# Old-form tiles, tile pairs by seven products, and the denominators of a fused attention and MLP kernel

## The chip, the cores and the metric

The kernel runs on one core of a Trainium2 chip. The metric is the device time of one execution, in microseconds (us). The engines are TensorE (PE in the profile; its weight loads are PEld), VectorE (DVE), ScalarE (ACT), GpSimd (POOL) and SyncE (SP), which here only issues DMAs.

## The reference

A linear attention with positive random features, and on its output an MLP with a gate. q, k and v are 8 x 8 x 576 x 64 (batch, heads, rows, head width), omega is 128 x 64, x has 4608 tokens of 512, the hidden width is 1536.

```python
    def phi(x):
        proj = np.einsum('bhsd,md->bhsm', x, omega)
        sq = np.sum(x * x, axis=-1, keepdims=True) / 2.0
        h = proj - sq
        h = h - np.max(h, axis=-1, keepdims=True)
        return np.exp(h) / np.sqrt(m)
    q_p, k_p = (phi(q_s), phi(k_s))
    kv = np.einsum('bhsm,bhsd->bhmd', k_p, v)
    z = np.sum(k_p, axis=2)
    num = np.einsum('bhsm,bhmd->bhsd', q_p, kv)
    den = np.einsum('bhsm,bhm->bhs', q_p, z)[..., None] + 1e-06
...
    g = x @ w_gate
    silu = g * (1.0 / (1.0 + np.exp(-g)))
    val = x @ w_val
    return (silu * val @ w_out).astype(np.float32)
```

## The kernel before

*Precision.* Each wide matmul of the MLP is three: its two operands are split into a rounded high part and a remainder (hi and lo, both 32 bits wide), and hi by hi, hi by lo and lo by hi are summed in PSUM. A split is a copy to hi on ACT and a subtraction to lo, on POOL for weights and hidden values, on DVE for x.

*Attention.* A group is 256 rows of one pair of heads; a batch has 9, the last of which holds the remaining 64 rows of all four pairs. A step n works on two groups: one of q and one of k, but two of k in the first 6 steps and two of q from step 66 on; there are 72 steps. What a step does, and where:

- `st_transpose`: PE transposes the rows (tile `pt`, L376), ACT copies the result to `x` (L384), POOL squares the rows for their norms (`sq`, L383).
- `st_project`: 16 products with omega (L399) into two PSUM banks, `pp0` and `pp1`.
- `st_max`: DVE sums the squares (L410), takes the maxima of `pp` (L417) and makes the bias `st` (L419, L420).
- `st_exp`: eight exponentials on ACT (L431) read `pp` and `st` and write the features `ph`.
- `k_accumulate`: features of k by v (L534), summed over a batch in `kvacc`. v has a 65th column of ones, so the denominators' vector z comes with it.
- `q_transpose` (`ptq`, L558, copied to `qt` on ACT), `q_mult` and `q_out`: the output of a q group. For batches below `BPOOL` = 4, `q_mult` multiplies `qt` by the 65 columns of kv (`po`, L575); DVE divides by the 65th (`xn`), and `q_out` transposes `xn` back (`xt`, L606). From batch `BPOOL` on, the denominators leave PE: POOL multiplies the features by a broadcast z (`q_den`: `jk`, L490 and L494), DVE sums and inverts, POOL scales the features (`q_norm`, L510) before they are transposed, and `q_out` writes the transposed output at once (`xt`, L613).
- behind either, x of a tile is split from PSUM into `xt[j]` in SBUF (L632 on ACT, L633 on DVE).

*PSUM.* There are eight banks of 128 x 512: four for the MLP (`ps_m`, and `pt` and half of `pp` in the first 25 steps), two in `ps_p` that `pp0`, `pp1`, `pt` and `xt` share in turn from step 25 on, one for `ptq`, `po` and the like, one for `kvacc`. Behind the attention the last four become `ps_w`, for the seven products.

*MLP.* The tokens are 9 tiles of 512, the hidden width 12 blocks of 128. In the **old form** the unit is a visit, one tile by a set of three blocks: 36 matmuls of 128x512 for the gates, 36 for the values (L647) and 36 for the sum into the output (`down`, L656; L680 adds it to `acc` on DVE), 108 in all. A tile takes four visits. `ROUNDS` gives tiles that are worked on together, so that a set of weights, once split, serves two or three tiles: (0, 1, 2), (3, 4), (5, 6), 28 visits. Tiles 7 and 8 go as a **pair** behind them (`last_round`): the pair and two blocks make a 2 x 2 product of blocks, done by seven products (L832) of sums and differences of weights (`load_seven`) and of x (`make_t`) in place of eight. Such a product is six matmuls of 128x512; a pair has six of these longer visits, with 2 x 7 x 6 = 84 of them and 48 of `down`. Their results are joined by L877 and L860 on DVE.

*Order.* All instructions are issued by one Python program, and each engine runs its own in that order. Up to step 25 the parts of a step follow in the order `CLOSE`, then in the order `GROUPED`, which has six slots `SHARE`. In a slot the generator `stream()` is drawn on for MLP work, until what was given has caught up with a curve, `course`. That curve is drawn like a rubber band between `upper` (MLP work whose x is there) and `lower` (work that must be done so that buffers of x, `NXB` pairs of them, come free), and ends `MARGIN` us short of all old-form work that can be had by then. Weights are read, unpacked (POOL, L278), split and stored to DRAM once, in `tick()`s spread over the steps by `marks`, and read from there later (`load_weights`).

The order of a step from the 25th on:

```python
    GROUPED = (
        st_project, q_transpose, lambda n: k_accumulate(n, 0),
        lambda n: k_accumulate(n, 1), st_max, st_exp, q_den,
        SHARE, SHARE, SHARE,
        lambda n: q_norm(n + 1), lambda n: st_transpose(n + 1), q_out, q_mult,
        SHARE, SHARE, SHARE,
    )
```

Of the kernel before, what the change touches and what calls it, by code (L numbers as in the profile page):

```python
# [23 lines left out]
def kernel(  # L24
# [11 lines left out]
    nc = tc.nc  # L36
# [40 lines left out]
    BPOOL = 4  # L77
# [162 lines left out]
    def new_weights(f, i, pool=None):  # L240
        hi, lo = (
            (pool or wpool).tile([P, DM], F32R, name=f"w{e}{f}_{i}", tag=f"w{e}{i}") for e in ("hi", "lo")
        )
        weights[f, i] = hi, lo
# [51 lines left out]
    def load_weights(f, i, pool=None):  # L296
        need(f, i)
        new_weights(f, i, pool)
# [164 lines left out]
    def load_z(n):  # L463

        for _, b, g, gr in slots(n, "q"):
            if g == 0 and b >= BPOOL:
                assert len(converted) == 3 * NF, "the raw weights' buffers are still needed"
                zt = att.tile([P, 2, 4, M], F32, name=f"zt{b}", tag="stw")
# [125 lines left out]

    xt = {}
    cols_done = [0]

    def q_out(n):
        n -= OLAG
        for _, b, g, gr in slots(n, "q"):  # L600
# [24 lines left out]
            for src, pr, j, o, w in parts_:  # L625
                if j not in xt:

                    while j - NXB >= 0 and not finished(j - NXB):
                        assert give(1), "the MLP waits for x, and x for the MLP"
# [28 lines left out]
    at_visit = [0]  # L658

    def finished(j):  # L660

        return at_visit[0] > last_visit[j]

# [5 lines left out]
    def down(j, k_, ht, wts, next_set, tt):  # L669
# [11 lines left out]
        if k_ == (NPF if j >= LASTA else NSET) - 1:  # L681
# [7 lines left out]
    def stream():  # L689

        todo = []
        for vi, (j, s_, k_) in enumerate(visits):
# [26 lines left out]
            if final:  # L719
                load_seven(0, 0)  # L720
# [17 lines left out]
            if final:  # L738
                load_seven(0, 1)
            at_visit[0] = vi + 1  # L740
# [3 lines left out]
        yield from last_round(todo)  # L744
# [10 lines left out]

    late_pools = {}
    sevens = {}
    ts = {}

    def load_seven(pf, i):  # L760

        win = late_pools["win"]
        raws_ = []
        for f in (2 * pf, 2 * pf + 1):
            raw = moe.tile([P, DM], F32, name=f"wraw{f}_{i}s", tag="wraw", bufs=3)
            nc.sync.dma_start(raw, wscr[f, i])
            raws_.append(raw)
        (a11, a12), (a21, a22) = ((r[:, 0:G], r[:, G:DM]) for r in raws_)
        s = win.tile([P, 4, G], F32, name=f"s{pf}_{i}", tag="s")
# [273 lines left out]
```

## Time and profile before

| what | value |
|---|---|
| runs | 1228.45, 1230.39, 1232.96 us; median 1230.39 |
| the profiled execution | 1232.11 us, of which the span, first to last instruction, is 1229.9 |
| granted clock of TensorE | 0.989, mean of the span |
| POOL's low halves of hidden values, L734 | 84 x 1319 ns |
| POOL's squares, L383 | 72 x 1066 ns |
| DVE's maxima, L417 | 144 x 684 ns |
| HBM | 80.02 MB read, 18.89 MB written |

The span in stretches: length, then the busy time of PE, PEld, DVE, ACT and POOL with the number of instructions, the granted clock, the busy share of the 16 DMA engines and GB/s.

```profile
0.00:25.00 25.00, 14.21 (x83) 11.90 (x84) 10.77 (x21) 9.76 (x25) 9.85 (x27) 0.78 0.66 158
25.00:145.00 120.00, 113.35 (x993) 101.56 (x993) 93.79 (x232) 91.77 (x274) 45.77 (x40) 0.95 0.57 143
240.00:1010.00 770.00, 765.27 (x4184) 618.89 (x4183) 324.81 (x627) 374.98 (x789) 346.73 (x289) 1.00 0.25 69
```

The first stretch is the start, before PE has work to do without waiting. The second has the steps in the order `CLOSE`. The third has the attention from some 10 steps behind that, with much MLP work in each step. The old form behind the attention begins near 1010, the pair's stage near 1050.

How to read rows: `L399 PE MATMUL pp<-omT,x ... x16 [2.47 <-ACT ph L431]` is a line, an engine, an operation, the tile written and the tiles read, with how many instructions, and in brackets how long the engine was idle ahead of it and which instruction it waited for. In the order of time, the first two numbers are the start and the length in us.

### The profile page before, as it was taken

The page shows a single profiled execution, that of the slowest core. Times are in us where ns is not written, and L with a number is a line of the kernel's source. Part 1 is how long each engine was busy: PE and PEld are TensorE (multiplying, and loading weights), DVE is VectorE, ACT ScalarE, POOL GpSimd, SP SyncE. Part 2 cuts the span into 40 slices and gives each one's busy share as a digit, 9 for nine tenths or more (in the row PEclk, how much of TensorE's full clock was granted, in tenths as well). Part 3 has the DMA queues.
Part 4 walks back from the last instruction along what each step waited for, and adds up shares of the span by engine and source line. Part 5 has one row for each costly group of instructions (what it writes and reads, how often), then busy time and mean ns, then how long its engine had stood idle before and what let it go on. Part 6 is the DMA issues. An engine that isn't in the chain of part 4 may idle for free. (4 is left out here: it accounts for less than half of the span.)

```text
span 1229.9 us, 18546 instructions
## 1 busy us (share of the span) xinstructions
PE 1193.3 (97%) x6777; PEld 978.9 (80%) x6777; DVE 607.8 (49%) x1192; ACT 624.6 (51%) x1387; POOL 549.3 (45%) x469
## 2 busy tenths in 40 slices
PE   6999999899999999999999999989999999999998
PEld 5888788688888888878888877877777787788886
DVE  4688767436556523433344434432334276545544
ACT  3778766543544425455754556434654423654431
POOL 3424333353444521335544654335556334656541
PEclk7899999999999999999999999999999999999999
DMA  6545644424326312232222221222111113321102
GB/s 148 138 121 141 177 137 142 117 78 142 90 68 181 90 35 73 61 78 61 72 62 61 78 56 44 61 51 60 46 42 43 43 43 77 96 52 52 52 18 69
DMA packets 158986, 100.13 MB, mean 81 GB/s; under 512 B 119824, under 2 KB 132144, under 8 KB 158896
## 3 DMA queue, kind: packets, MB, share of 16 engines
q1 hardware_dynamic: 158896, 98.95, 30.1%
q8 instruction: 54, 0.88, 0.3%
q14 instruction: 36, 0.29, 0.1%
HBM read 80.02 MB, written 18.89 MB: 80 GB/s over the span
## 5 line engine op out<-in xcount | busy, mean ns | idle before, releaser
L431 ACT ACTIVATE ph<-pp,st 128x128 f32<-128x128 f32 x576 | 158.6, 382 | 31.8 <-DVE st L420 30.9
L249 POOL TENSOR_TENSOR wlo<-wraw,whi 128x512 fp32r<-128x512 f32 x93 | 121.8, 1319 | 107.5 <-ACT whi L248 107.1
L383 POOL TENSOR_TENSOR sq<-nat 128x512 f32<-128x512 f32 x72 | 76.7, 1066 | 191.9 <-DMA nat<-in_k_dram 143.2
L680 DVE TENSOR_TENSOR acc<-o,acc 128x512 f32<-128x512 f32 x124 | 84.6, 687 | 116.5 <-PE o L656 116.2
L656 PE MATMUL o<-whi,hh 128*128 128x512 f32 x336 | 135.5, 403 | 3.8 <-ACT hh L733 2.0
L647 PE MATMUL v<-xh,whi 128*128 128x512 f32 x336 | 134.5, 400 | 0.7 <-DVE acc L680 0.7
L647 PE MATMUL g<-xh,whi 128*128 128x512 f32 x336 | 134.6, 401 | 0.0
L656 PE MATMUL o<-whi,hl 128*128 128x512 f32 x336 | 132.3, 394 | 2.3 <-POOL hl L734 2.3
L647 PE MATMUL g<-xl,whi 128*128 128x512 f32 x336 | 131.7, 393 | 0.5 <-DVE xl L633 0.5
L656 PE MATMUL o<-wlo,hh 128*128 128x512 f32 x336 | 131.6, 392 | 0.0
L647 PE MATMUL v<-xh,wlo 128*128 128x512 f32 x336 | 131.4, 391 | 0.0
L647 PE MATMUL g<-xh,wlo 128*128 128x512 f32 x336 | 131.3, 392 | 0.0
L647 PE MATMUL v<-xl,whi 128*128 128x512 f32 x336 | 131.2, 391 | 0.0
L734 POOL TENSOR_TENSOR hl<-sl,hh 128x512 fp32r<-128x512 f32 x84 | 110.5, 1319 | 41.8 <-ACT hh L733 41.3
L417 DVE TENSOR_REDUCE st<-pp 128x4 f32<-128x512 f32 x144 | 93.5, 684 | 54.2 <-PE pp L399 54.2
L733 ACT CAST hh<-sl 128x512 fp32r<-128x512 f32 x84 | 52.1, 626 | 108.7 <-DVE sl L730 108.5
L248 ACT CAST whi<-wraw 128x512 fp32r<-128x512 f32 x93 | 57.4, 625 | 92.2 <-PE v L647 54.1
L410 DVE TENSOR_REDUCE st<-sq 128x8 f32<-128x512 f32 x72 | 49.1, 682 | 105.0 <-POOL sq L383 105.0
L399 PE MATMUL pp<-omT,x 64*128 64x128 f32 x1152 | 98.3, 296 | 2.4 <-ACT x L384 1.2
L399 PEld LDWEIGHTS pp<-omT,x 64*128 64x128 f32 x1152 | 81.2, 196 | 22.8 <-issue 13.9
L730 DVE TENSOR_TENSOR sl<-v,sl 128x512 f32<-128x512 f32 x84 | 57.3, 686 | 72.3 <-PE v L647 70.0
L494 POOL TENSOR_TENSOR jk<-ph,zt 128x512 f32<-128x512 f32 x32 | 41.1, 1290 | 103.6 <-ACT ph L431 86.8
(200 smaller groups left out, 2448.3 us busy)
## 6 DMA issues: line engine op xcount, KB each, us to landing
wraw<-wscr SPq DMA_DIRECT2D x93, 256.0 KB, 2.7
wscr<-wc SPq DMA_DIRECT2D x36, 256.0 KB, 2.2
out_dram<-acc SPq DMA_DIRECT2D x72, 128.0 KB, 2.4
nat<-in_k_dram SPq DMA_DIRECT2D x64, 128.0 KB, 3.3
v<-in_v_dram SPq DMA_DIRECT2D x64, 128.0 KB, 3.4
nat<-in_q_dram SPq DMA_DIRECT2D x64, 128.0 KB, 2.7
st<-in_moe_w_gate_dram SPq DMA_DIRECT2D x12, 512.0 KB, 5.1
st<-in_moe_w_val_dram SPq DMA_DIRECT2D x12, 512.0 KB, 4.4
```

The costliest lines, as they stand in the source:

```text
L248: nc.scalar.copy(hi, raw)
L249: nc.gpsimd.tensor_tensor(lo, raw, hi.bitcast(F32), op=ALU.subtract)
L383: nc.gpsimd.tensor_tensor(sq, nat, nat, op=ALU.mult)
L399: nc.tensor.matmul(pp[hh][:, i, c, :], x[r, i, c * P : (c + 1) * P], omT[r], start=True, stop=True)
L417: nc.vector.tensor_reduce(st[:, 1, :, :, hh], pp[hh], axis=AX.X, op=ALU.max, negate=True)
L431: nc.scalar.activation(ph[:, c, hh * M : (hh + 1) * M], pp[hh][:, i, c, :], AF.Exp, bias=st[:, 3, i, c, hh : hh + 1], scale=1.0,)
L647: nc.tensor.matmul(ps, a_[:, ws], b_[:, c, :], start=n == 0, stop=n == 3 * NC - 1)
L656: nc.tensor.matmul(ps, a_[:, ts_], b_, start=first and n == 0, stop=last and n == 2)
L680: nc.vector.tensor_tensor(a_, po, a_, op=ALU.add)
L730: nc.vector.tensor_tensor(h, pv, h, op=ALU.mult)
L733: nc.scalar.copy(hh, h)
L734: nc.gpsimd.tensor_tensor(hl, h, hh.bitcast(F32), op=ALU.subtract)
```

## The change

1. *Old form and pairs.* `ROUNDS` keeps tiles 0 to 2, 12 visits. Tiles 3 and 4, 5 and 6, 7 and 8 become three pairs by seven products, one behind the other, all behind the attention (`pair_rounds` in place of `last_round`). `MARGIN` goes from 25 to 45 us, and `course` has no lower bound any more.
2. *x of the pairs.* `q_out` copies x of tiles 3 to 8 from PSUM to `xo` (ACT) and stores it to DRAM (`x_dram`), in place of the split into SBUF. The first pair's is read back and split in chunks of 128x512 by `first_x`, in front of the rest of the old-form work behind the attention. A later pair's is read back and added up in the second visit of the pair ahead of it (`next_x`), and split, 128x1024 at a time, in the second half of that pair's last visit (`split_x`), each factor behind the product that reads its predecessor.
3. *Buffers.* The factors' high and low parts have one buffer each. Hidden values, sums and products of the pairs use the buffers of x, of the old form and of `acc`. `NXB` is 3; the broadcast z has a buffer of its own. The products come in the order 1, 5, 6, 3, 7, 2, 4, as before; blocks go forward in the first and third pair and backward in the second, so that a change of pairs needs no new weights.
4. *Denominators.* `BPOOL` goes from 4 to 2: batches 2 and 3 (18 q groups) take the way by POOL too.

```diff
-    ROUNDS = [range(0, 3), range(3, 5), range(5, 7)]
-
-    LASTA, LASTB = 7, 8
+    ROUNDS = [range(0, 3)]
+    PAIRS = [(j, j + 1) for j in range(3, len(TILES), 2)]
     NPF = NF // 2
-    MARGIN = 25.0
-    NXB = 4
+    MARGIN = 45.0
+    NXB = 3
...
-    BPOOL = 4
+    BPOOL = 2
...
         upper[n] = cum[vi] if n > whole[1] else 0.0
-        lower[n] = max([0.0] + [cum[last_visit[j - NXB] + 1] for j in begun if j >= NXB and begun[j] <= n])
-    lower = np.minimum(lower, upper)
...
-                zt = att.tile([P, 2, 4, M], F32, name=f"zt{b}", tag="stw")
+                zt = att.tile([P, 2, 4, M], F32, name=f"zt{b}", tag="zt")
...
+    x_dram = {j: dram.tile([P, NPAIR, T], F32, name=f"xs{j}") for pair in PAIRS for j in pair}
...
+                if j in x_dram:
+                    xo = att.tile(list(src.shape), F32, name=f"xo{b}_{g}_{j}", tag="xo", bufs=3)
+                    nc.scalar.copy(xo, src)
+                    nc.sync.dma_start(x_dram[j][:, pr, o : o + w], xo)
+                    continue
...
+    ORDER = (1, 5, 6, 3, 7, 2, 4)
+    ORDER_B = [PROD[n][1] for n in ORDER]
...
+    def next_x(r):
+
+        for half, names in ((0, ("b11", "t1")), (1, ("b21", "b22"))):
+            for j, name in zip(PAIRS[r], names):
+                nc.sync.dma_start(ahead[name], x_dram[j][:, half * CH : (half + 1) * CH, :])
+        yield
+        for o, a, b in (("t3", "b22", "t1"), ("t1", "t1", "b11"), ("t2", "b22", "t1"), ("t4", "b21", "t2")):
+            for c in range(CH):
+                nc.vector.tensor_tensor(ahead[o][:, c], ahead[a][:, c], ahead[b][:, c], op=ALU.subtract)
+                yield
...
+    def split_x(name):
+        hi, lo = factors[name]
+        nc.scalar.copy(hi, ahead[name])
+        nc.vector.tensor_tensor(lo, ahead[name], hi.bitcast(F32), op=ALU.subtract)
...
+        for vi, (r, k_, pf) in enumerate(pair_visits):
+            then = pair_visits[vi + 1] if vi + 1 < len(pair_visits) else None
+            new_w = then and then[2] != pf
+            new_x = then and then[0] != r
+            if k_ == 1 and r + 1 < len(PAIRS):
+                prep = next_x(r + 1)
...
+                for n in ORDER:
+                    product({5: c, 3: c, 2: d}.get(n, a), n, wts, n in (1, 5, 2))
...
+                    if new_x and i == 1:
+                        split_x(PROD[n][1])
+                    yield US7
+                    if n in (5, 3, 2, 4) and one_down():
+                        yield MM2
...
-    late_pools["mt"] = make_t()
-    for _ in late_pools["mt"]:
-        give(1.0)
+    new_factors()
+    for _ in first_x():
+        give(1.5)
```

What this does to the order of instructions is shown at three places. A line number of the changed kernel can differ from that of before for the same code by 3 to 8 here (L396 and L399 are both the projections).

**First place: PE, step 51, between its projections and the next step's.** `pp` are the projections, `ptq` the transposes of q's features, `kvacc` the k features by v, `pt` the next step's transposes, `xt` an output group; `g`, `v` and `o` are MLP work. Before:

```order
L399 MATMUL pp_51_6225<-omT,x_6165 128x128
L558 MATMUL ptq_7_6234<-ident,ph_49_5950 128x128 x4
L534 MATMUL kvacc_0_6090<-v_95,ph_49_5955 128x65 x4
L647 MATMUL v_6_6269<-xh_2566,whi_1_5971 128x512
L647 MATMUL v_7_6287<-xh_2566,whi_1_5995 128x512
L376 MATMUL pt_6301<-ident,nat_5909 128x128 x4
L613 MATMUL xt_6_6311<-qt_6_6088,kvr_1_4781 64x256 x2
L647 MATMUL v_8_6321<-xh_2566,whi_1_6037 128x512
L647 MATMUL g_6_6339<-xh_4864,whi_0_5878 128x512
L399 MATMUL pp_52_6359<-omT,x_6306 128x128
```

Of each `v` and `g` the first of twelve matmuls is shown. Now:

```order
L396 MATMUL pp_51_4664<-omT,x_4621 128x128
L656 MATMUL o_1_3_4713<-whi_2_3660,hl_5_4387 128x512
L647 MATMUL v_3_4743<-xh_1600,whi_1_3202 128x512
L554 MATMUL ptq_8_4774<-ident,ph_50_4561 128x128 x4
L530 MATMUL kvacc_0_4551<-v_96,ph_50_4566 128x65 x4
L647 MATMUL v_4_4818<-xh_1600,whi_1_3250 128x512
L373 MATMUL pt_4726<-ident,nat_4435 128x128 x4
L611 MATMUL xt_6_4736<-qt_6_4549,kvr_1_3488 64x256 x2
L647 MATMUL v_4_4818<-xh_1600,wlo_1_3251 128x512
L396 MATMUL pp_52_4764<-omT,x_4731 128x128
```

Before, 24 MLP matmuls stood ahead of the transposes `pt` and 24 behind them. Now 13 stand right behind the projections, 2 between `kvacc` and `pt`, and 3 ahead of the next projections.

**Second place: DVE in the half visit at a pair's end.** `c`, `a` and `d` are the products' PSUM banks, `o` that of `down`. Before, in a half visit of the one pair (`sl` are the gates' and hidden values):

```order
L877 TENSOR_TENSOR c_1_10776<-c_1_10736,u_1_10768 128x512
L860 TENSOR_TENSOR sl_1_10617<-c_1_10776,sl_1_10617 128x512
L680 TENSOR_TENSOR acc_1_10526<-o_1_1_10781,acc_1_10526 128x512
L877 TENSOR_TENSOR c_3_10795<-a_1_10735,m_1_10752 128x512
L860 TENSOR_TENSOR sl_3_10619<-c_3_10795,sl_3_10619 128x512
L877 TENSOR_TENSOR c_0_10806<-d_1_10737,m_1_10744 128x512
L860 TENSOR_TENSOR sl_0_10616<-c_0_10806,sl_0_10616 128x512
L680 TENSOR_TENSOR acc_2_10557<-o_1_2_10811,acc_2_10557 128x512
L860 TENSOR_TENSOR sl_2_10618<-a_1_10735,sl_2_10618 128x512
```

Now, where the first pair ends; L923 are the sums, L905 the hidden values, L674 the additions to `acc`, L813 the splits, in which `late` is a full factor:

```order
L813 TENSOR_TENSOR b11lo<-late_7492,b11hi 128x1024
L674 TENSOR_TENSOR acc_0_7901<-o_4_0_8857,acc_0_7901 128x512
L813 TENSOR_TENSOR t1lo<-late_7492,t1hi 128x1024
L923 TENSOR_TENSOR late_7496<-c_1_8837,late_7496 128x512
L813 TENSOR_TENSOR t2lo<-late_7493,t2hi 128x1024
L905 TENSOR_TENSOR sl1k<-late_7496,sl1k 128x512
L813 TENSOR_TENSOR b22lo<-late_7493,b22hi 128x1024
L813 TENSOR_TENSOR t3lo<-late_7494,t3hi 128x1024
L813 TENSOR_TENSOR b21lo<-late_7494,b21hi 128x1024
L905 TENSOR_TENSOR sl2k<-a_1_8836,sl2k 128x512
L813 TENSOR_TENSOR t4lo<-late_7495,t4hi 128x1024
```

Seven splits stand between the evacuations; all but `t4lo` are ahead of the one of bank `a` (`sl2k`).

**Third place: POOL where the third batch's q groups begin.** `sq` are the squares, `wc` an unpacked weight. Before:

```order
L278 TENSOR_TENSOR wc_0_2318<-st_0_2211,wc_0_2318 128x512
L734 TENSOR_TENSOR hl_2_2189<-sl_2_2001,hh_2_2188 128x512
L383 TENSOR_TENSOR sq_2449<-nat_2147 128x512
L278 TENSOR_TENSOR wc_1_2424<-st_1_2316,wc_1_2424 128x512
L383 TENSOR_TENSOR sq_2558<-nat_2256 128x512
```

Now:

```order
L490 TENSOR_TENSOR jk_1_1966<-ph_25_1828,zt_1802 128x512
L506 TENSOR_TENSOR ph_25_1828<-ph_25_1828,dj_1_1968 128x512
L380 TENSOR_TENSOR sq_2243<-nat_1926 128x512
L275 TENSOR_TENSOR wc_0_2102<-st_0_1991,wc_0_2102 128x512
L490 TENSOR_TENSOR jk_2_2094<-ph_26_1956,zt_1802 128x512
L275 TENSOR_TENSOR wc_1_2165<-st_1_2100,wc_1_2165 128x512
L506 TENSOR_TENSOR ph_26_1956<-ph_26_1956,dj_2_2096 128x512
L380 TENSOR_TENSOR sq_2345<-nat_2041 128x512
```

Each step has two more operations on POOL here, a product `jk` and a scaling of `ph`.

More of the change, by code (lines that the diff above doesn't have):

```diff
@@ new lines, in first_x @@
+    def first_x():
+        win = late_pools["win"]
+        for c in range(CH):
+            x = {}
+            for name, j, o in (("b11", 0, 0), ("b21", 0, CH), ("t1", 1, 0), ("b22", 1, CH), ("t3", None, None)):
+                x[name] = win.tile([P, T], F32, name=f"first_{name}{c}", tag="first", bufs=5)
+                if j is not None:
+                    nc.sync.dma_start(x[name], x_dram[PAIRS[0][j]][:, c + o, :])
+            yield
+            for name, a, b in (
+                ("b11", None, None),
+                ("b22", None, None),
+                ("b21", None, None),
+                ("t3", "b22", "t1"),
+                ("t1", "t1", "b11"),
+                ("t2", "b22", "t1"),
+                ("t4", "b21", "b22"),
+            ):
+                place = {"t2": "b22", "t4": "b21"}.get(name, name)
+                if a is not None:
+                    nc.vector.tensor_tensor(x[place], x[a], x[b], op=ALU.subtract)
+                hi, lo = (y[:, c] for y in factors[name])
+                nc.scalar.copy(hi, x[place])
+                nc.vector.tensor_tensor(lo, x[place], hi.bitcast(F32), op=ALU.subtract)
+                yield
```

203 lines of the change are left out of this document (91 added, 112 removed).

## The prediction

> **What bounds the kernel now.** I read the page's busy shares first, then the granted clock and PE's idle time by stage, then the chain that ended last.
>
> ```profile
> PE 1193.3 (97%) x6777; PEld 978.9 (80%) x6777; DVE 607.8 (49%) x1192; ACT 624.6 (51%) x1387; POOL 549.3 (45%) x469
> 25.00:120.00 95.00, 89.61 (x822) 81.72 (x822) 72.09 (x179) 71.44 (x219) 34.14 (x31) 0.93 0.53 132
> 145.00:240.00 95.00, 89.02 (x600) 74.01 (x599) 64.43 (x145) 57.40 (x139) 32.95 (x26) 1.00 0.48 137
> 145.00:1010.00 865.00, 854.28 (x4782) 692.90 (x4781) 389.23 (x772) 432.38 (x927) 379.67 (x315) 1.00 0.28 77
> 1010.00:1050.00 40.00, 37.62 (x163) 29.98 (x162) 23.79 (x32) 13.77 (x25) 20.75 (x16) 1.00 0.29 74
> 1050.00:1230.00 180.00, 173.88 (x764) 142.56 (x762) 90.18 (x137) 76.91 (x138) 93.26 (x73) 1.00 0.20 54
> ```
>
> A row of the second to sixth kind is a stretch, its length, then busy time of PE, PEld, DVE, ACT, POOL, the granted clock and DMA. PE is busy 97% of the span, so PE work that goes is time that goes, unless PE waits more. What the reader has to see is where it waits already: from 145 to 1010 it is idle 865.00 - 854.28 = 10.7 us, and 95.00 - 89.02 = 6.0 of these fall in the first 95 us. There the attention runs with little MLP beside it; from 240 on some 10 us of MLP lie in every attention step, and almost nothing waits.
>
> ```profile
> 1070.07 1.36 PE c L832 x6
> 1212.87 12.25 PE o L656 x54
> ```
>
> In the chain that ended last, pieces of six 512-wide matmuls follow each other without a gap: 105 of them from the first row's start to the second's. That is 142.8 / 105 / 6 = **0.2267 us a matmul**.
>
> **The change, part by part.** *Fewer products.* A tile pair in the old form is 2 x 4 visits of 108 matmuls, 864; by seven products it is 6 visits of 84 + 48, 792. Two pairs more change form: 144 matmuls go, 144 x 0.2267 = **-32.6 us**, all on the bounding engine.
>
> *Denominators.* For batches 2 and 3 (18 groups), the 65-wide products and two transposes give way to two wider products.
>
> ```profile
> 494.15 0.38 PE L606 MATMUL xt<-ident,xn 128*128 128x128 f32 x2
> 494.37 1.00 PE L575 MATMUL po<-kvr,qt 128*128 128x65 f32 x8
> 495.18 0.48 PE L656 MATMUL o<-whi,hh 128*128 128x512 f32 x1
> 534.32 0.65 PE L613 MATMUL xt<-qt,kvr 128*64 128x256 f32 x4
> 534.90 0.50 PE L656 MATMUL o<-whi,hh 128*128 128x512 f32 x1
> ```
>
> The first three rows are a group before (495.18 - 494.15 = 1.03 us), the last two the later batches' form (0.58): 18 x 0.45 = **-8.1 us**. POOL gets 1.29 + 1.04 us for each of these groups:
>
> ```profile
> L494 POOL TENSOR_TENSOR jk<-ph,zt 128x512 f32<-128x512 f32 x32 | 41.1, 1290 | 103.6 <-ACT ph L431 86.8 <-ACT sl L714 8.0 <-PE xt L606 7.1
> L510 POOL TENSOR_TENSOR ph<-ph,dj 128x512 f32<-128x512 f32 x36 | 37.3, 1040 | 31.5 <-DVE dj L500 23.2 <-PE v L647 3.9 <-PE xt L613 1.8
> ```
>
> That is 42 us. I cost it at nothing by itself, since POOL is a third busy in the stage (32.95 of 95); what is queued behind a waiting norm is POOL's own next squares and low halves, then the query transposes on PE. Without that cover each group would cost up to one POOL operation, 1.3 us, 23 in all.
>
> *A thinner cover for the attention.* This is the term I trust least. The old form now has 12 visits, not 28, beside the attention. From the order, the 46 steps from step 26 on have 23 MLP matmuls each (5.2 us). Before, steps 27 to 34 had 22, the 37 steps behind them 36 and more. So the stretch 145:240 of before is the pattern of the whole attention now.
>
> ```profile
> L399 PE MATMUL pp<-omT,x 64*128 64x128 f32 x144 | 14.6, 285 | 1.5 <-DVE xl L633 0.8 <-ACT x L384 0.7
> ```
>
> A step has 16 of these, so that stretch is 9 steps and its 6.0 us of idle time 0.66 a step. Why PE waits there is seen in the order of time, PE first, then ACT:
>
> ```profile
> 200.70 1.16 PE L399 MATMUL pp<-omT,x 64*128 64x128 f32 x16
> 201.79 0.66 PE L558 MATMUL ptq<-ident,ph 128*128 128x128 f32 x4
> 207.70 0.66 PE L376 MATMUL pt<-ident,nat 128*128 128x128 f32 x4 [0.46 <-ACT ph L431]
> 211.10 1.16 PE L399 MATMUL pp<-omT,x 64*128 64x128 f32 x16
> 219.60 0.66 PE L376 MATMUL pt<-ident,nat 128*128 128x128 f32 x4 [2.47 <-ACT ph L431]
> 226.50 1.16 PE L399 MATMUL pp<-omT,x 64*128 64x128 f32 x16
> 485.74 1.16 PE L399 MATMUL pp<-omT,x 64*128 64x128 f32 x16
> ```
>
> ```profile
> 205.99 2.17 ACT L431 ACTIVATE ph<-pp,st 128x128 f32<-128x128 f32 x8 [2.29 <-DVE st L420]
> 217.89 2.17 ACT L431 ACTIVATE ph<-pp,st 128x128 f32<-128x128 f32 x8 [1.22 <-DVE st L420]
> 229.42 2.17 ACT L431 ACTIVATE ph<-pp,st 128x128 f32<-128x128 f32 x8 [0.49 <-DVE st L420]
> 489.56 2.17 ACT L431 ACTIVATE ph<-pp,st 128x128 f32<-128x128 f32 x8
> ```
>
> Projections, transposes and outputs share two PSUM banks, so the next transposes wait until six of the eight exponentials have read theirs: they start 1.71 us behind the first (207.70 - 205.99, 219.60 - 217.89). Counted from the end of the projections (1.09 us behind their start, 201.79 - 200.70), the bank is free after 5.9, 7.4 and 3.5 us in the three dense steps and after 4.4 in the sparse one. PE's own work in between, counted off the order at the spacing of such rows, is 5.1 us in the dense steps of before and 5.0 now. From the transposes to the next projections it falls from 2.6 to 2.3, in half the steps to 1.2 to 1.9, and ACT needs until 199.05 + 0.38 - 197.88 = 1.6 us for both copies:
>
> ```profile
> 197.88 0.60 PE L376 MATMUL pt<-ident,nat 128*128 128x128 f32 x4
> ```
>
> ```profile
> 198.57 0.59 ACT L384 COPY x<-pt 128x512 f32<-128x512 f32 x1 [0.58 <-PE pt L376]
> 199.05 0.38 ACT L632 CAST xh<-xt 128x256 fp32r<-128x256 f32 x1
> ```
>
> So a little more waits than before: 0.66 + 0.1 = 0.76 a step, x 46 = 35, less the 10.7 that the stretch had: **+24 us**. Ends: 0.25 a step, if the bank is always free as in the sparse step (+1; and if all waits are hidden -11), and 1.5, if every second step were like the one at 211 (+58).
>
> *Changing pairs.* Twice, DVE and ACT must split seven factors of 128x1024 in half a visit, in front of the last evacuation (the order's second place).
>
> ```profile
> L822 DVE TENSOR_TENSOR t1l<-t2f,t1h 128x512 fp32r<-128x512 f32 x2 | 3.5, 1772 | 0.0
> L822 DVE TENSOR_TENSOR t3l<-t4f,t3h 128x512 fp32r<-128x512 f32 x2 | 1.4, 684 | 0.1
> L860 DVE TENSOR_TENSOR sl<-a,sl 128x512 f32<-128x512 f32 x6 | 4.1, 689 | 2.5 <-PE a L832 2.5
> ```
>
> Twice the width is an estimated 1.37 us (2 x 0.684) up to 3.5. In order stand six splits, three additions, three accumulations and four products, 6 x 1.37 + 10 x 0.69 = 15.1 us, from 3.2 us into the half visit (one product, a copy and a cast on ACT). The bank comes free at 18.3; PE wants it after twelve pieces of 1.36 us, at 16.3. That is 2 us, or 7 if four POOL operations hold DVE up. I take 3: **+6 us** for both, from 0 to 14.
>
> The Trainium skill, SBUF — State Buffer, section "Who interferes with whom", says that a VectorE instruction with two SBUF inputs and a GpSimd instruction that reads SBUF exclude each other for a whole instruction. By that rule, which speaks against more POOL work and against these splits, the term would go to its upper end, 14. The two forms of one subtraction above, 684 and 1772 ns, agree with it.
>
> *The rest at nothing.* The first pair's factors are read from DRAM and split under 201 old-form matmuls, 45 us, behind the attention; its 22 VectorE operations are 15 us free and 39 held up at the prices above; what stands there now costs 40.00 - 37.62 = 2.4 us of idle time, and I keep that (to +4). Stores and loads of x lie on SP behind a lead of two steps.
>
> **Sum:** -32.6 - 8.1 + 24 + 6 = -10.7. The profiled execution took 1232.1 us (span 1229.9), 1.7 over the median of the runs, 1230.4; so 1221 for it, and **1220 us** as a median.
>
> **Rivals.** *The cover holds.* Waits stay at 0.25 a step: -32.6 - 8.1 + 1 + 6 = -34, 1197 us. For it: between 25 and 120 the steps follow each other faster still with PE busy 94%. Against: those steps had more PSUM banks. 20%.
>
> *The two banks become the bound* (the other side). If the bank is free 7.4 us behind the projections in every second step, the wait is 1.5 a step: -40.7 + 58 + 6 = +24, 1254 us. It decides from 1.0 a step on, where the gain is eaten, and from 1.1 the time is over 0.5% longer. For it: weight conversions now lie beside the whole attention, POOL is busier. Against: conversions are spread thinner than in 145:240. 13%.
>
> *POOL's queue holds the query transposes up:* 23 us on the forecast, 1243. 5%.
>
> *PE's clock falls.*
>
> ```profile
> 15.00:20.00 5.00, 1.68 (x8) 1.66 (x8) 4.08 (x11) 2.64 (x10) 0.46 (x1) 0.50 1.01 274
> 215.00:220.00 5.00, 2.53 (x17) 2.13 (x15) 4.97 (x8) 2.78 (x9) 3.57 (x3) 1.00 0.31 90
> 830.00:835.00 5.00, 5.00 (x19) 3.57 (x19) 0.29 (x1) 1.88 (x4) 0.00 (x0) 0.69 0.00 0
> ```
>
> A wait of 2.5 us left the clock at 1.00, two waits behind each other cost a third of the next 5 us. If the 46 steps ran at the 0.93 of 25:120, their 430 us would take 30 more: 1250. 2%. The Trainium skill, TensorE: Matmul & The Clock Gate, section "HAM oscillation — how this bites in real kernels", has the clock halved once idle gaps pass about 3.4 us; the three rows agree.
>
> That the products do not go is excluded by the order, which has 3672 of these matmuls, before 3816.
>
> **Numbers.** Forecast 1220, with waits of 0.4 to 1.0 a step 1203 to 1232: 60%. The range takes in the first rival and stops short of the worst of the second: 1197 to 1246. A measurement of this kernel can tell about 0.5% from no change, so under 1224.2 is faster and over 1236.5 slower. Faster: the first rival and some 57% of the forecast's case, 0.54; slower: the three other rivals, 0.20, and 0.02 of the forecast's case, with larger stalls at the pairs' changes, 0.22; the same 0.24.
>
> **What would show it.** PE's count of 512-wide matmuls down by 144; in the attention, idle time of PE of about 0.76 us a step, most of it in front of the transposes with ACT's exponentials named, the rest in front of the projections with ACT's copies; the attention over near 590 us; at two places 180 us apart a wait of some 3 us on a VectorE evacuation. I am wrong if waits in the attention are under 0.4 or over 1.0 a step, if the query transposes name POOL, or if the pairs' stage loses more than 14 us.

## The result, and the profile after

The changed kernel takes 1267.3 us (1261.1 to 1278.1), the kernel before 1231.3 beside it: ratio 1.0304, 95% interval 1.0231 to 1.0378. It is slower by 36 us where 11 less was forecast, and lies outside the range. The spans of the two profiled executions differ by as much, 1265.9 - 1229.9 = 36.0.

The page of after, busy time by engine:

```profile
PE 1187.1 (94%) x6537; PEld 960.6 (76%) x6537; DVE 733.2 (58%) x1338; ACT 669.9 (53%) x1507; POOL 656.1 (52%) x557
```

Two stretches of each kernel follow, cut at the same points of the program: from the first MLP matmul beside the attention to the attention's last output, then the pairs' stage. Before:

```profile
131.10:992.30 861.20, 849.42 (x4770) 688.39 (x4769) 384.35 (x778) 436.93 (x940) 378.88 (x315) 1.00 0.29 79
1034.98:1225.00 190.02, 188.79 (x829) 154.83 (x827) 94.85 (x144) 81.49 (x146) 100.33 (x79) 1.00 0.20 54
```

After:

```profile
133.50:660.20 526.70, 474.82 (x2928) 365.71 (x2929) 315.46 (x619) 307.64 (x758) 301.12 (x258) 0.95 0.38 106
704.30:1261.00 556.70, 550.20 (x2412) 453.13 (x2412) 294.61 (x454) 253.89 (x444) 290.00 (x227) 1.00 0.22 61
```

PE waits 526.70 - 474.82 = 51.9 us in the attention, before 861.20 - 849.42 = 11.8. The granted clock there is 0.95. Summed over stretches of 5 us, one minus the clock makes 23.9 us, before 1.8 (the "clock's loss" below). The program has 1068 wide (512-column) matmuls in this stretch after, 2817 before; at 0.2267 us each, the span's difference is made up so:

| part | forecast | measured |
|---|---|---|
| 144 wide matmuls fewer | -32.6 | -32.6 |
| PE's other work in the attention (denominators) | -8.1 | 474.82 - 23.9 - 242.1 = 208.8, before 209.0: -0.2 |
| waits in the attention | +24 | +40.1 |
| clock | 0 | +22.1 |
| pairs' stage above its matmuls | +6 | 556.7 - 546.8 = 9.9, before 2.3: +7.6 |
| start, and old form behind the attention | 0 | +2.4, -3.3 |

So the loss is in the attention. What PE waited for there, first before and then after (us in total, times, longest):

```profile
PE pt L376 <- ACT ph L431: 3.8, 4, 2.5
```

```profile
PE pt L373 <- ACT ph L428: 41.0, 23, 4.5
PE pp L396 <- DVE xl L633: 4.1, 2, 3.0
PE kvacc L530 <- ACT ph L428: 3.8, 1, 3.8
PE pp L396 <- ACT xo L626: 3.2, 3, 2.0
```

The transposes wait for the exponentials, as forecast. What makes these late is in the exponentials' own group, before and after:

```profile
L431 ACT ACTIVATE ph<-pp,st 128x128 f32<-128x128 f32 x576 | 158.6, 382 | 31.8 <-DVE st L420 30.9
```

```profile
L428 ACT ACTIVATE ph<-pp,st 128x128 f32<-128x128 f32 x576 | 158.3, 386 | 93.5 <-DVE st L417 88.0
```

They take as long as before, but ACT waits 88 us for the bias, in place of 31. One of the longest waits shows why. VectorE in the order of time, in step 42, whose projections ended at 328.0:

```profile
327.16 0.69 DVE L494 TENSOR_REDUCE dj<-jk 128x4 f32<-128x512 f32 x1 [2.37 <-POOL jk L486]
327.76 1.00 DVE L271 TENSOR_SCALAR wc<-st 128x512 int32<-128x512 int32 x1
...
329.18 0.65 DVE L273 SCALAR_TENSOR_TENSOR wc<-st,wc 128x512 f32<-128x512 uint32 x1
329.76 1.53 DVE L269 SCALAR_TENSOR_TENSOR st<-st,wc 128x512 int32<-128x512 int32 x1
331.32 1.42 DVE L271 TENSOR_SCALAR wc<-st 128x512 int32<-128x512 int32 x1
332.65 1.28 DVE L414 TENSOR_REDUCE st<-pp 128x4 f32<-128x512 f32 x2
333.85 0.67 DVE L407 TENSOR_REDUCE st<-sq 128x8 f32<-128x512 f32 x1
334.45 0.15 DVE L416 SCALAR_TENSOR_TENSOR st<-st 128x8 f32<-128x8 f32 x1
334.52 0.68 DVE L273 SCALAR_TENSOR_TENSOR wc<-st,wc 128x512 f32<-128x512 uint32 x1
335.12 0.15 DVE L417 SCALAR_TENSOR_TENSOR st<-st 128x8 f32<-128x8 f32 x1
```

ACT and PE behind it:

```profile
335.37 2.17 ACT L428 ACTIVATE ph<-pp,st 128x128 f32<-128x128 f32 x8 [8.33 <-DVE st L417]
```

```profile
337.08 1.11 PE L373 MATMUL pt<-ident,nat 128*128 128x128 f32 x4 [4.51 <-ACT ph L428]
```

VectorE had just stood 2.37 us for a product of the denominators (`jk`) that POOL had not made. Then unpacking of a weight (`wc`) stands ahead of the maxima (L414), and a sum of squares for a later step (L407) and one more unpacking operation (L273) between the maxima and the end of the bias (L416, L417). **Start** below is the time from the end of a step's projections to its first exponential, averaged over the steps 26 to 70 of the order of time: 4.22 us after; before, 2.70 in the sparse steps 40 to 64 and 3.52 in the dense ones 26 to 33. Of the 4.22 us, 1.05 are unpacking (and 0.14 VectorE's waits for it), 0.95 are sums of squares or VectorE's waits for POOL's squares.

### The profile page after: what moved, and what is told of

The parts are those of the page before. It is cut to its first block, busy times and chain, and to the rows that moved or that the text cites. A ratio compares the mean times of both kernels' runs of the same rounds, so it can differ in the third digit from the quotient of the medians.

```text
span 1265.9 us, 18943 instructions
## 1 busy us (share of the span) xinstructions
PE 1187.1 (94%) x6537; PEld 960.6 (76%) x6537; DVE 733.2 (58%) x1338; ACT 669.9 (53%) x1507; POOL 656.1 (52%) x557
## 5 line engine op out<-in xcount | busy, mean ns | idle before, releaser
L674 DVE TENSOR_TENSOR acc<-o,acc 128x512 f32<-128x512 f32 x156 | 106.6, 684 | 70.1 <-PE o L656 69.9
L842 POOL TENSOR_TENSOR wlo<-wraw,whi 128x512 fp32r<-128x512 f32 (+1 forms) x64 | 68.6, 1073 | 120.2 <-ACT whi L841 119.9
L842 POOL TENSOR_TENSOR wlo<-s,whi 128x512 fp32r<-128x512 f32 x64 | 95.9, 1515 | 58.3 <-ACT whi L841 21.1
L414 DVE TENSOR_REDUCE st<-pp 128x4 f32<-128x512 f32 x144 | 93.6, 683 | 45.1 <-PE pp L396 45.0
L396 PE MATMUL pp<-omT,x 64*128 64x128 f32 x1152 | 111.6, 307 | 7.4 <-DVE xl L633 4.1
L396 PEld LDWEIGHTS pp<-omT,x 64*128 64x128 f32 x1152 | 92.5, 205 | 29.0 <-ACT xo L626 9.2
L373 PE MATMUL pt<-ident,nat 128*128 128x128 f32 x288 | 51.4, 300 | 42.8 <-ACT ph L428 41.0
L246 POOL TENSOR_TENSOR wlo<-wraw,whi 128x512 fp32r<-128x512 f32 x59 | 77.1, 1311 | 22.5 <-ACT whi L245 17.9
L275 POOL TENSOR_TENSOR wc<-st,wc 128x512 f32<-128x512 f32 x36 | 49.1, 1363 | 70.0 <-DVE wc L273 50.4
L407 DVE TENSOR_REDUCE st<-sq 128x8 f32<-128x512 f32 x72 | 49.0, 680 | 54.1 <-POOL sq L380 54.0
L506 POOL TENSOR_TENSOR ph<-ph,dj 128x512 f32<-128x512 f32 x54 | 57.2, 1062 | 39.6 <-DVE dj L496 34.0
L530 PE MATMUL kvacc<-v,ph 128*128 128x65 f32 x512 | 71.7, 281 | 4.3 <-ACT ph L428 3.8
L656 PE MATMUL o<-whi,late 128*128 128x512 f32 x192 | 74.5, 389 | 0.0
L530 PEld LDWEIGHTS kvacc<-v,ph 128*128 128x128 f32 x512 | 68.4, 204 | 7.4 <-ACT ph L428 4.0
L919 ACT COPY late<-a 128x512 f32<-128x512 f32 x72 | 42.0, 584 | 49.0 <-PE a L851 46.2
L841 ACT CAST whi<-wraw 128x512 fp32r<-128x512 f32 (+1 forms) x64 | 32.9, 514 | 64.7 <-PE a L851 47.8
```

Of the source, the lines that this page charges most:

```text
L246: nc.gpsimd.tensor_tensor(lo, raw, hi.bitcast(F32), op=ALU.subtract)
L373: nc.tensor.transpose(pt[:, i, c * P : (c + 1) * P], nat[:, i, c].rearrange("p h d -> p (h d)"), ident)
L396: nc.tensor.matmul(pp[hh][:, i, c, :], x[r, i, c * P : (c + 1) * P], omT[r], start=True, stop=True)
L414: nc.vector.tensor_reduce(st[:, 1, :, :, hh], pp[hh], axis=AX.X, op=ALU.max, negate=True)
L530: nc.tensor.matmul(acc[:, 2 * (pr % 2) + hh, :], ph[:, c, hh * M : (hh + 1) * M], vt[:, 2 * c + j if gr is None else c, hh, :], start=firs ...
L656: nc.tensor.matmul(ps, a_[:, ts_], b_, start=first and n == 0, stop=last and n == 2)
```

## The experiments

Each edit is to the changed kernel unless another is named. In the table, idle time and clock's loss are those of the attention beside MLP work, in the one execution that was profiled.

| run | us | ratio to before, 95% | idle | clock | start |
|---|---|---|---|---|---|
| after | 1267.3 | 1.0304 (1.0231 to 1.0378) | 51.9 | 23.9 | 4.22 |
| e1 no unpacking | 1256.5 | 1.0200 (1.0161 to 1.0240) | 51.2 | 22.2 | 4.02 |
| e2 BPOOL 4 | 1258.5 | 1.0224 (1.0195 to 1.0252) | 43.4 | 25.6 | 4.11 |
| e3 pt's bank | 1252.0 | 1.0177 (1.0146 to 1.0208) | 50.0 | 17.1 | 4.17 |
| e4 MARGIN 85 | 1270.2 | 1.0318 (1.0288 to 1.0348) | 50.9 | 27.2 | 3.82 |
| e5 EARLY 40 | 1254.6 | 1.0182 (1.0146 to 1.0218) | 33.6 | 13.7 | |
| e6 EARLY 50 | 1250.4 | 1.0144 (1.0108 to 1.0180) | 25.0 | 13.4 | |
| e7 two pairs | 1266.6 | 1.0282 (1.0247 to 1.0316) | 41.8 | 12.0 | |
| e8 pt's and xt's banks | 1245.3 | 1.0100 (1.0060 to 1.0139) | 45.4 | 22.2 | 5.16 |
| e9 st with two buffers | 1254.6 | 1.0176 (1.0143 to 1.0209) | 43.7 | 23.9 | 3.78 |
| e10 e9 and e1 | 1221.0 | 0.9908 (0.9881 to 0.9935) | 25.2 | 5.6 | 2.95 |
| e11 e9 and e8 | 1236.7 | 1.0038 (1.0020 to 1.0056) | 40.9 | 15.3 | 4.54 |
| e12 two pairs, even | 1231.4 | 1.0000 (0.9972 to 1.0028) | 21.4 | 10.2 | 3.48 |
| e13 e12 and e8 | 1222.4 | 0.9920 (0.9889 to 0.9951) | 18.6 | 6.8 | 3.26 |
| e14 e11, BPOOL 4 | 1229.6 | 0.9969 (0.9949 to 0.9989) | 32.9 | 13.7 | 3.88 |
| e15 before, e10's edits | 1216.9 | 0.9874 (0.9840 to 0.9908) | 3.9 | 0.0 | 2.62 |
| e16 e13, BPOOL 2 | 1232.8 | 1.0001 (0.9976 to 1.0027) | 28.4 | 17.0 | 4.16 |

The intervals of e1, e2, e4 and e7 overlap with that of after: by themselves these four do not show a gain or a loss clear of the noise.

**e1: unpacking out of VectorE's queue.** The kernel leaves out five VectorE operations for 27 weights; so do e10 and e15.

```diff
-            nc.vector.tensor_scalar(u, u, E_LO, E_HI, op0=ALU.max, op1=ALU.min)
+            if f < FA:
+                nc.vector.tensor_scalar(u, u, E_LO, E_HI, op0=ALU.max, op1=ALU.min)
...
```

> The changed kernel without the five VectorE operations that unpack a weight, for the 27 weights that are unpacked beside the later attention (those weights get other values; nothing else is left out). In the changed kernel the transposes pt wait 41.0 us for exponentials. If the exponentials are late because unpacking stands ahead of the maxima in VectorE's queue (theory Q), the waits that contain such operations shrink: laid over one another they account for 20.7 us, so pt's waits fall to about 20, the clock's loss by half (some 10 us), and the time to about 1237 us. If the cover is too thin whatever VectorE does (theory A: shared banks and too little MLP work in a step), at most 10 us go: 1257 to 1267.

11 us went, but not the waits. VectorE and PE in e1's table of waits:

```profile
DVE st L412 <- POOL sq L385: 96.0, 45, 6.1
PE pt L378 <- ACT ph L433: 46.2, 27, 6.2
```

VectorE, free of unpacking, now stood 96 us at the sums (54.0 after) for squares that POOL had not made; the start hardly moved. Alone, theory Q fails.

**e2: the denominators back on TensorE.**

```diff
-    BPOOL = 2
+    BPOOL = 4
```

> BPOOL back to 4: batches 2 and 3 have their denominators on TensorE again, all else as changed. If the denominators' chain through POOL and VectorE makes the waits (theory D), the stretch from 145 to 365 us loses its waits, about 20 of them with the clock, and the time falls to about 1250. If not, TensorE gets 18 x 0.45 = 8 us more work, part of which fills waits: 1267 to 1276.

Nearly 9 us less, where by the change's own sum it should be 8 more. The waits fell by 8.5 us and did not go: not the main cause, but no gain either.

**e3: another bank for the transposes.**

```diff
-        pt = (ps_moe if n <= EARLY else ps_proj)(f"pt_{n}", [P, 2, G])
+        pt = (ps_moe if n <= EARLY else ps_att)(f"pt_{n}", [P, 2, G])
```

> From step 26 on the transposes pt are written to the bank of ptq in place of the two banks of the projections, all else as changed. Theory A (shared banks): pt no longer waits for exponentials; the next projections do, but with a whole step of other work, some 8 us, ahead of them, against exponentials that end 5.9 us behind the projections in the mean and 9.5 at worst. PE's idle time in the attention falls from 67 us to about 30, the clock stays at 1.00 for most of it, and the time is 1205 to 1230. Theory Q (VectorE's queue is simply too slow for a step this short): the wait moves to the projections and half of it stays, about 1245.

The wait moved to the outputs, which still share the projections' banks:

```profile
PE xt L611 <- ACT ph L428: 37.6, 25, 4.5
```

**e4: less cover.**

```diff
-    MARGIN = 45.0
+    MARGIN = 85.0
```

> MARGIN 85 in place of 45: 40 us of old-form MLP work go from beside the attention to behind it, nothing is added or left out. Theory A: each step from 26 on has 0.87 us less cover, some 30 steps wait 0.87 longer, +26 us, and the clock loses 8 more: about 1300. Theories Q and D: the work is only moved, 1262 to 1275.

20 matmuls a step in place of 23, and the idle time is the same; other waits took the place of pt's, first of all those of the query transposes for POOL's scaling, the prediction's third rival (1.0 us after):

```profile
PE ptq L554 <- POOL ph L506: 20.0, 17, 3.1
PE kvacc L530 <- ACT ph L428: 17.0, 11, 3.3
PE pt L373 <- ACT ph L428: 7.8, 7, 1.9
```

Within this range the thickness of the cover is not what sets the sum of the waits.

**e5, e6: MLP work later and thicker**, here with 40; e6 has 50.

```diff
-        upper[n] = cum[vi] if n > whole[1] else 0.0
+        upper[n] = cum[vi] if n > 40 else 0.0
...
-    EARLY = whole[1]
+    EARLY = 40
```

Where the order changes from CLOSE to GROUPED, one group of q is left without its scaling (one POOL operation of 1.06 us). The steps up to `EARLY` also use the MLP's banks for `pt` and half of `pp`, so the banks change along with the order.

> The changed kernel with EARLY at 40 in place of 24: steps up to 39 run in the order CLOSE with no MLP work beside them, and the same 12 old-form visits lie beside the steps from 40 on, some 31 matmuls in each in place of 23. Nothing is added or left out. In the changed kernel a step from 26 on loses 1.1 us to waits and 0.5 to the clock, a step in the order CLOSE before it 0.26 and 0.25. Theory P (a step that mixes attention with a little MLP work is what loses, whatever engine is late): 16 steps lose 0.5 in place of 1.6 and the others about half: -18 and -25, 1225 us. Theory E (the engines beside TensorE are too busy with denominators, unpacking and copies): steps in the order CLOSE, which have less time, wait more than mixed ones, 1.7 us each: 1270 or more.

> The same with EARLY at 50: some 42 matmuls in each mixed step. Theory P: 26 steps lose 0.5 in place of 1.6, the rest nearly nothing, as with 36 to 48 matmuls before: -30 and -30, about 1207. Theory E: slower than with 40, 1280.

Theory P fails. In e6 the 21 mixed steps have 42 matmuls each and still lose (25.0 + 13.4) / 21 = 1.8 us, with all unpacking beside them. Ahead of the first MLP matmul, idle time is 40.1 us in place of 15.9 and the clock's loss 29.2 in place of 11.9, so the 26 added steps in the order CLOSE lose (24.2 + 17.3) / 26 = 1.6 us each, as theory E has it. Both runs are faster all the same, by 13 and 17 us: waits and clock together are level with after in e5, and what fell is PE's other work, by some 18 us. No run here explains that.

**e7: two pairs**, with before's lower bound of `course`; `xo` takes the buffers of `jk`, and the broadcast z, as before, those of the raw weights.

```diff
-    ROUNDS = [range(0, 3)]
-    PAIRS = [(j, j + 1) for j in range(3, len(TILES), 2)]
+    ROUNDS = [range(0, 3), range(3, 5)]
+    PAIRS = [(j, j + 1) for j in range(5, len(TILES), 2)]
...
-    NXB = 3
+    NXB = 4
...
-    BPOOL = 2
+    BPOOL = 4
```

> Five tiles in the old form (rounds 0 to 2 and 3 to 4, 20 visits), two pairs, BPOOL at 4, four buffers of x: 72 wide matmuls fewer than before, 72 more than in the changed kernel. From the order: six steps have 144 matmuls of MLP work, the steps from the 40th on 24 each with no unpacking beside them. Theory P: the steps with 24 lose 1.6 us as in the changed kernel, some 28 of them, +40 on 1231 - 16 + 5: about 1258. If what loses is the unpacking of weights beside the attention, they lose nothing: 1220.

1266.6: slower than either theory gave. In the 28 steps from the 44th on, without unpacking, the start is 4.05 us: sums of squares (1.1 us with VectorE's waits for them) and the denominators' sums (0.9) stand there now.

**e8: no shared banks.**

```diff
-        pt = (ps_moe if n <= EARLY else ps_proj)(f"pt_{n}", [P, 2, G])
+        pt = (ps_moe if n <= EARLY else ps_att)(f"pt_{n}", [P, 2, G])
...
-            po = (ps_att if n + OLAG < EARLY else ps_proj)(f"xt{b}_{g}", [P, G])
+            po = (ps_att if n + OLAG < EARLY else ps_moe)(f"xt{b}_{g}", [P, G])
```

> As in e3 the transposes pt go to the bank of ptq, and the outputs xt too leave the projections' banks, for the four banks of the MLP. Then only the next projections wait for exponentials, with all of a step's MLP work ahead of them. Theory A (shared banks): idle time in the attention falls from 67 us to 25, the clock's loss from 36 to 15, 1267 - 60 = 1207. If it is the exponentials' lateness itself, the wait moves on to the projections, as it moved to xt in e3: 1245 to 1255.

With no bank shared with the projections, PE waits for ScalarE's copies, which stand behind the late exponentials in ScalarE's queue. Theory A, which gave 1207, fails as the main cause:

```profile
PE pp L396 <- ACT x L381: 16.4, 14, 4.0
```

Still, the run takes 22 us off, more than e1 or e9. The profiled execution, 1255.8 us, is 10 over the median, so its row understates that. Its idle time fell by 6.5 us, while PE's other work in the attention is 198.5 us in place of 208.8; what the banks have to do with the latter no run shows.

**e9 and e10: the sums held back, without and with the unpacking.**

```diff
-        st = att.tile([P, 4, 2, CH, 2], F32, name=f"st_{n}", tag="st", bufs=6)
+        st = att.tile([P, 4, 2, CH, 2], F32, name=f"st_{n}", tag="st" if n <= EARLY else "sv", bufs=6 if n <= EARLY else 2)
```

> The changed kernel with two buffers in place of six for the biases st of the steps from 26 on. A sum of squares then cannot be put three steps ahead, between a step's maxima and its bias; it waits for the exponentials of two steps before to be done with their buffer. Nothing is added or left out. In the changed kernel these sums and the waits for POOL's squares take 0.9 us between the projections and the exponentials, 18 us of the waits of pt. Theory L (what loses is that the exponentials start late, 4.2 us behind the projections in place of 2.7 in the sparse steps of before, by work of others in VectorE's queue; unpacking alone was no cure in e1 since the sums then waited longer): -18, and half as much by the clock, 1240. If the start stays late by something else: 1260 to 1267.

> As e9, and without the five unpacking operations of VectorE for 27 weights, whose values are other ones then. Theory L: the exponentials start some 2.5 to 2.8 us behind the projections, as in the sparse steps of before, with the same 23 matmuls a step; of 41 us of waits for exponentials 35 go, and most of the clock's 24: 1267 - 35 - 20 = 1212. If 23 matmuls a step are too thin a cover all the same, the waits stay above 25 us and the time above 1235.

These decide. e9 gains 13 us, half of what theory L gave; e10 gains 46, the whole loss and 10 more. Waits of e9, then of e10, and e10's attention:

```profile
PE pt L373 <- ACT ph L428: 29.9, 19, 5.7
DVE st L407 <- POOL sq L380: 15.3, 6, 6.0
```

```profile
PE pt L378 <- ACT ph L433: 14.1, 15, 2.9
ACT ph L433 <- DVE st L422: 43.4, 38, 4.6
```

```profile
133.80:613.10 479.30, 454.08 (x2928) 351.57 (x2929) 231.66 (x481) 309.28 (x757) 289.49 (x258) 0.99 0.42 116
```

e1 and e9 gave 11 and 13, both together 46: two things stand ahead of the exponentials, and with one gone the other fills its place. The clock came back with the waits, 5.6 us lost in place of 23.9.

**e15: the control**, the kernel before with e10's edits (five buffers of st up to step 24, for want of room).

> The control: the kernel before with e10's two edits, that is without the five unpacking operations for 27 weights (whose values are other ones then) and with two buffers of st behind step 24. Theory L: before, PE waits 6 us for exponentials in all, since 36 and more matmuls cover them; at most 10 us go, 1221 to 1231. If less work on VectorE makes any version of this kernel faster, as much goes as between the changed kernel and e10: about 1185.

15 us less, more than the 10 that theory L allowed and far from the 46 of a general gain. So 31 of e10's 46 us are the changed kernel's own. Cured of both, the two kernels are 4 us apart, with overlapping intervals, in place of 36; but the change was to gain 11, and even so it gains nothing. The attention of e15:

```profile
127.50:976.60 849.10, 845.22 (x4770) 686.27 (x4770) 300.82 (x643) 438.12 (x940) 372.25 (x315) 1.00 0.29 80
```

**e11, e14: kernels that leave nothing out**; e14 is e11 with `BPOOL = 4`.

> e8's banks and e9's buffers together, nothing left out. Theory L: the sums leave VectorE's queue (0.95 idle and 0.6 busy of 5.18 us in e8), the copies on ScalarE come earlier by as much, and of e8's 49 us of idle time in the attention half goes: 1225. If not, as e8, 1245.

> e11 with BPOOL at 4, the denominators of batches 2 and 3 on TensorE, nothing left out. If the 8 us of TensorE's work that the change takes away count as soon as the exponentials are earlier: 1237 + 8 = 1245. If the denominators' operations on POOL and VectorE stand in the way of the exponentials by as much, as e2 says of the changed kernel: 1230 to 1237.

e11 takes 31 us off the changed kernel, less than expected. e14 takes 7 more: with the denominators on POOL the kernel is slower by nearly as much as they were to save.

**e12, e13, e16: two pairs, evenly.** Tiles 3 and 4 stay in the old form, but their x goes through DRAM as well and is split as soon as tiles 0 and 1 give up their buffers, so that `course` needs no lower bound; st as in e9, `BPOOL` 4. e13 adds e8's banks, e16 goes back to `BPOOL` 2.

```diff
+            if j in ROUNDS[0] and vi == last_visit[j] and j + 3 in ROUNDS[1]:
...
+                    nc.sync.dma_start(raw, x_dram[j + 3][:, c, :])
+                    hi, lo = (t[:, c] for t in xt[j + 3])
+                    nc.scalar.copy(hi, raw)
+                    nc.vector.tensor_tensor(lo, raw, hi.bitcast(F32), op=ALU.subtract)
```

> A version meant to be fast: five tiles in the old form and two pairs (72 wide matmuls fewer than before, -16 us), x of tiles 3 and 4 through DRAM too, so that the 20 visits lie evenly beside the attention, 42 matmuls in each step from 26 on; BPOOL at 4, st with two buffers. If 36 to 48 matmuls a step cover the exponentials as they do before: idle time and clock as before (29 and 14 us), one pair change more (+4): about 1220. If what loses is the mixture with unpacking, now spread over all steps, it loses in each: 25 to 40 more, 1245 to 1260.

> e12 (two pairs, 20 visits spread evenly, BPOOL 4, two buffers of st) with e8's banks, nothing left out. In e12 PE waits 20 us for exponentials at pt and loses 10 by the clock. If the other banks spare it these, as e11's did beside e9: idle time 22 to about 12, the clock's loss to 5, about 1217. If the copies on ScalarE take their place, as in e8: 1231.

> e13 with BPOOL at 2, nothing left out: the denominators of batches 2 and 3 on POOL. If they cost TensorE nothing: e13 less 8 us, about 1209. If they delay the exponentials as much as they save: the same as e13.

e12 is level with before. e13 beats both kernels: 1222.4 us, ratio 0.992, interval 0.9889 to 0.9951. e16 gives the gain back. In its steps 26 to 44 the exponentials start at 5.42 us, in e13's at 3.62: unpacking takes 2.29 there in place of 1.53, and VectorE waits 0.71 for the unpacking's other engines in place of 0.25. e13's attention, then e16's:

```profile
126.20:786.40 660.20, 641.57 (x3861) 515.40 (x3860) 337.74 (x673) 382.68 (x857) 311.55 (x263) 0.99 0.37 100
```

```profile
129.70:802.10 672.40, 643.98 (x3768) 507.60 (x3769) 355.42 (x675) 382.09 (x861) 359.50 (x304) 0.97 0.36 100
```

POOL is busy 48 us longer. Less the clock's loss, PE's work is 643.98 - 17.0 = 627.0 us in e16 and 641.57 - 6.8 = 634.8 in e13: 7.8 less, as the change meant it. Idle time takes 9.8 back and the clock 10.2.

## Why the prediction was wrong

- *Fewer products, -32.6:* right.
- *Denominators, -8.1:* PE's other work fell by 1 us in after beside e2, by 5 in e11 beside e14 and by 7.8 in e16 beside e13, so the saving was there in full in one pair of three; why it shrank in the others is open. The step that failed: POOL's 42 us "at nothing by itself, since POOL is a third busy". The same three pairs put the way over POOL 9, 7 and 10 us behind; the intervals of the last two pairs are apart, those of the first overlap.
- *A thinner cover, +24, waits of 0.76 us a step:* this step failed most: "So the stretch 145:240 of before is the pattern of the whole attention now." That the wait is the exponentials' time less the cover was the right mechanism; the start was carried over from eight steps of before, 3.52 us, and it became 4.22, since the denominators and the sums that wait for POOL's squares joined the unpacking on VectorE. Waits rose by 40.1, to 51.9 / 46 = 1.13 a step, over the 1.0 that was named as a sign of being wrong. e10 shows about what the cover alone costs: with a start of 2.95, shorter than the 3.52 carried over, 25.2 us of idle time are left, 13 more than before; the other 27 went with the late start.
- *The clock, 0, with a rival at 2%:* +22.1, the largest miss against its chance. "A wait of 2.5 us left the clock at 1.00" was one row, taken as the rule; the last section sets 14 waits beside it. No run sets the clock alone; that it follows the waits rests on e10 and e13, where both fall together, and it follows them loosely: e2 lost less to waits and a little more to the clock.
- *Changing pairs, +6:* +7.6 for the stage, near in number by luck. At neither change did PE wait: the 128x1024 splits took 1.22 us, less than the lowest price of 1.37, and the stretches of the splits (876.9 to 891.9, 1058.5 to 1073.6) lie in the second and fourth row below. The waits stand in the first pair's first two visits (first row), the longest of them, 2.60 us, for a VectorE operation that stood behind the subtractions for the next pair's x (`next_x`), a term that the sum did not have; 1.5 us more for ScalarE's copies follow in the third row:

```profile
704.30:750.00 45.70, 40.91 (x177) 32.66 (x177) 27.19 (x38) 21.28 (x38) 26.71 (x22) 1.00 0.37 110
870.00:900.00 30.00, 30.00 (x135) 24.82 (x134) 24.09 (x31) 15.22 (x22) 8.56 (x6) 1.00 0.28 88
900.00:930.00 30.00, 28.46 (x124) 22.92 (x123) 17.75 (x27) 13.33 (x25) 18.16 (x14) 1.00 0.40 113
1050.00:1080.00 30.00, 30.00 (x134) 24.85 (x133) 21.01 (x29) 16.13 (x24) 7.21 (x5) 1.00 0.07 18
749.54 0.50 PE L851 MATMUL a<-t4hi,whi 128*128 128x512 f32 x1 [2.60 <-DVE sl2k L923]
```

- *The rival of the two banks*, 1254 us and from 1.0 us a step: its price was the nearest, and its mechanism was a part: e3 and e8 took the banks away, gained 15 and 22 us, and the waits moved on; e10 gained 46 with the banks shared. *The cover holds*, at 0.25 us a step, is ruled out by 1.13. *POOL's queue* held the query transposes up for 1.0 us in all.
- *Its argument against, "conversions are spread thinner than in 145:240":* true (1.05 us of a start in place of 1.56), and no help, since other work took the room.

## What to carry to other kernels

When work moves behind a short dependent chain, price the chain first: read in the queue of each engine on it what stands ahead of the links, of later steps too, and expect one such thing to fill the place of another, so that taking away one alone shows nothing. A stretch of the old kernel stands for the new one only if all engines of the chain carry the same load there. And short waits have a second price when the clock follows them.

## What was not expected of the hardware

The clock fell behind some single waits of PE of 2 us and less. PE in the order of time, after:

```profile
223.22 1.16 PE L396 MATMUL pp<-omT,x 64*128 64x128 f32 x8 [2.01 <-ACT xo L626]
...
224.79 0.63 PE L647 MATMUL v<-xh,wlo 128*128 128x512 f32 x1
...
228.28 0.39 PE L647 MATMUL v<-xh,wlo 128*128 128x512 f32 x1
```

Behind 2.01 us of waiting a matmul takes 0.63 us, in place of 0.39, for some 3.4 us, in which the granted clock is 0.50:

```profile
224.44:227.85 3.41, 3.41 (x9) 2.65 (x10) 3.41 (x7) 0.06 (x1) 2.70 (x3) 0.50 0.59 166
```

Length alone does not tell. There are 14 waits of 1.66 us and more in the attention beside MLP work. At 10 of them the clock fell during the wait or within 2 us behind it; at four, of 2.01, 2.15, 2.52 and 2.89 us, it did not. The one of 2.01 us:

```profile
529.22 0.66 PE L373 MATMUL pt<-ident,nat 128*128 128x128 f32 x4 [2.01 <-ACT ph L428]
525.00:530.00 5.00, 2.99 (x17) 2.13 (x18) 1.70 (x5) 3.49 (x10) 1.27 (x1) 1.00 0.00 0
530.00:535.00 5.00, 5.00 (x35) 3.72 (x33) 3.08 (x8) 1.36 (x3) 2.08 (x2) 1.00 0.32 82
```

The Trainium skill, TensorE: Matmul & The Clock Gate, section "HAM oscillation — how this bites in real kernels", puts the limit at gaps of about 3.4 us; here the measurement differs, and the prediction had leaned on its agreement. Already the third of its rows, 830 to 835 of before, stood behind waits of 2.02 and 1.31 us, neither of them that long.

The same unpacking operation took 1.42 us in step 42's queue above and 0.41 elsewhere (L271 in both), which the prediction's prices left out:

```profile
488.63 0.41 DVE L271 TENSOR_SCALAR wc<-st 128x512 int32<-128x512 int32 x1
```

The trace shows what goes with it. L267 and L271, the same kind of operation, ran 72 times in after: 50 took 0.41 to 0.43 us, and 13 of these overlap in time with an operation of POOL; the other 22 took 0.83 to 1.50, and all of them do. So it is with the two operations of the bias, which are in the chain itself: 116 took 0.13 to 0.19 us, and 28 took 0.31 to 1.27, each beside an operation of POOL, 24.7 us together. In e16 43 of the bias's operations took 0.24 us and more, in e13 29. The maxima, which read PSUM, took 0.66 to 0.70 us all 144 times, 90 times beside an operation of POOL. The rows of the bias and of the maxima in after (shortest, middle and longest time in ns, start of the first and of the last in us):

```profile
L414 DVE TENSOR_REDUCE st<-pp x144: 660/681/695, 13.1 to 632.5; 128x4 f32<-128x512 f32 x144
L416 DVE SCALAR_TENSOR_TENSOR st<-st x72: 148/158/1193, 15.8 to 633.2; 128x8 f32<-128x8 f32 x72
L417 DVE SCALAR_TENSOR_TENSOR st<-st x72: 134/160/1274, 16.5 to 633.4; 128x8 f32<-128x8 f32 x72
```

So work on POOL seems to reach the exponentials by a second way, besides the order of the queues; no run tells the two ways apart.

Busy shares of VectorE, 49% before and 58% after, show nothing of such delays.
